# One operand in PSUM for the last batch's Strassen sums, q's pair sums and low halves of the later heads, with a new order table

## The chip, the cores and the metric

The kernel runs on one core of a Trainium2 chip. A core has TensorE (PE: matmuls; PEld is its weight loads), VectorE (DVE), ScalarE (ACT), GpSimd (POOL) and SyncE (SP, which issues the DMAs here). SBUF is the large on-chip memory, PSUM the small one of eight banks that TensorE writes and that DVE and ACT also read and write (no POOL instruction of this kernel does). The metric is the device time of one execution in microseconds, as the median of several runs.

## The reference

```python
B, H, S, D = 4, 8, 1152, 64              # q, k, v: (B, H, S, D), float32
q_pool = q.reshape(B, H, S // 2, 2, D).mean(axis=3)           # 576 queries
scores = (q_pool @ k.transpose(0, 1, 3, 2)) / np.sqrt(D)
scores = scores - scores.max(-1, keepdims=True)
attn = np.exp(scores); attn = attn / (attn.sum(-1, keepdims=True) + 1e-09)
x = (attn @ v).transpose(0, 2, 1, 3).reshape(B * 576, H * D)  # 2304 x 512
gate = 1.0 / (1.0 + np.exp(-(x @ w_gate)))                    # 512 x 1536
return (gate * (x @ w_val)) @ w_out                           # 1536 x 512
```

## The kernel before

**Numbers.** Most operands are split into a high part in the matmul's reduced float32 format and a low part, the rest. A product is three matmuls: high by high, high by low, low by high. So every operand needs a high copy (ACT) and a subtraction for the low part (POOL or DVE).

**Attention.** The 32 heads run one after the other, in pairs that share an x tile. `head_operands` (from line 479) loads a head's q and k, forms the sum of each pair of queries on POOL (q_sum, line 504, 64x576), its high half twice on ACT (line 509), the low half (line 514, on DVE for heads 16 to 31, on POOL for the earlier ones), k's high halves on ACT (line 524) and its low halves (line 530; the second of the two on DVE for heads 16 to 31, by KLD). `maxima` multiplies transposed scores on TensorE (line 553) and reduces them on DVE (line 559) into pm, the maximum of each query. The 576 queries are two halves of 288 columns. For each, `half` multiplies scores (line 671), ACT takes exponentials (675, 704), DVE forms the low part el (707), TensorE multiplies by v (714, 718), and POOL adds up the denominators (736, 743, 746). `normalise` divides (transposes and reciprocal on DVE, a product on POOL) and splits the result into x (lines 842 and 846).

**Gated layer.** After the heads of a batch come that batch's gate, value and output products, line 970, mixed into the heads of the next batch. Weights come from DRAM in tiles wg and wo (lines 1005, 984). The gated low part of g is formed on POOL (1209). In the last batch, after which no heads are left to mix with, the gate and value products use Strassen's scheme with seven products instead of eight. `differences` forms four differences of blocks of x (T1 to T4): sums on DVE (line 882), high halves on ACT (871), low halves on DVE (875). `combinations` forms four sums of weight blocks (S1 to S4): two full sums of 128x512 (line 1028), four mixes of 128x256 (1031), both on DVE with all operands in the tile kr, then highs on ACT (1044) and lows on POOL (1048). `seven` multiplies (line 1082), keeps a first result (ACT, 1100), adds others to it (DVE, 1092 and 1128), and `two_rows` takes tanh (1141), the product with the gate (1151) and its split (1155, 1158).

**Order.** Nothing is scheduled by the compiler. Every operation is registered with `pl.op` (engine, estimated time, due time, what it follows, which tiles it takes), and at the end `Plan.placed` puts all operations in the order of a stored table, ORDER; a second one, PLACES, says which buffer of its tag each tile gets. Each engine runs its own instructions in that order, and semaphores between engines follow from the tiles. So an instruction that waits holds up all that stands behind it on its engine. Of the buffers that matter here there are 8 PSUM banks (tag b), 1 kr, 1 vr, 2 wo, 3 wg, 3 sg, 2 r, 2 y, 2 t and 1 acc.

## Time and profile before

| what | value |
|---|---|
| median of 3 runs | 918.13 us (917.62 to 918.35) |
| the profiled execution | 919.11 us |
| its span | 917.3 us |
| PE busy | 894.9 us, 98% |
| DVE busy | 749.6 us, 82% |
| POOL busy | 714.1 us, 78% |
| ACT busy | 671.2 us, 73% |

The span runs from the first to the last instruction in the trace; the profiled execution's own time is 1.8 us more. PE's busy time counts a pipelined matmul until its end, so a busy PE can still have issued less than it could; the number of matmuls in a window tells more. DVE, POOL and ACT are busy for most of the time beside it and matter where PE waits for them.

### The profile page before, as it was taken

What the parts mean: (1) busy time and instruction counts of PE and PEld (TensorE: products, weight loads), DVE (VectorE), ACT (ScalarE), POOL (GpSimd) and SP (SyncE); (2) the same over time, 40 slices, a digit from 0 to 9 for tenths busy, and PEclk for the clock granted to TensorE, in tenths of its full rate; (3) what the DMA queues carried; (4) which work ended last, traced back from release to release, by engine and by line L of the source; (5) the groups of instructions that cost most, each with busy time, mean ns of one, the idle gap of its engine ahead of it and who ended that gap; (6) DMA issues with size and microseconds to landing.
All of it is one profiled execution on the core that took longest, in us unless ns stands there. A gap on an engine that the chain in (4) does not pass through costs nothing.

```text
span 917.3 us, 18691 instructions
## 1 busy us (share of the span) xinstructions
PE 894.9 (98%) x6251; PEld 869.0 (95%) x6251; DVE 749.6 (82%) x1605; ACT 671.2 (73%) x1747; POOL 714.1 (78%) x711
## 2 busy tenths in 40 slices
PE   7999999999999999999999999999999989999998
PEld 6888889999999999999999999999999979889997
DVE  7888869898998979788687778878787888998964
ACT  4999989999998776778876777787778646544421
POOL 7676658998998889899889889989798768745521
PEclk9999999999999999999999999999999989999999
DMA  7899887978868666536345453555544213456313
GB/s 193 255 282 286 266 222 227 276 247 251 294 203 262 200 171 190 165 104 185 123 153 154 105 168 119 181 176 166 148 132 151 88 54 108 144 185 209 136 64 126
DMA packets 57856, 164.40 MB, mean 179 GB/s; under 512 B 16864, under 2 KB 21216, under 8 KB 52000
## 3 DMA queue, kind: packets, MB, share of 16 engines
q1 hardware_dynamic: 57600, 162.91, 57.5%
...
q10 hardware_dynamic: 160, 0.30, 0.1%
...
## 4 chain that ended last, share of the span: by engine, by line
PE 83%; DVE 9%; DMA 3%; issue 2%; POOL 1%; ACT 1%; SPq 0%; DVEq 0%; ACTq 0%; POOLq 0%
PE bank L970 37%; PE bank L671 16%; PE bank L553 8%; PE bank L689 7%; PE bank L718 6%; PE bank L714 6%; PE bank L1082 2%; DVE kr L1031 2%; DVE kr L1028 1%; DMA wo<-wo_d 1%; PE bank L794 1%; DVE bank L1128 1%; DMA vt<-wg_d 1%; DVE sg L1092 1%; DVE el L707 1%
## 5 line engine op out<-in xcount | busy, mean ns | idle before, releaser
L970 PE MATMUL bank<-x,wg 128*128 128x288 f32 x1728 | 289.5, 296 | 0.5 <-DVE pm L559 0.5
L970 PEld LDWEIGHTS bank<-x,wg 128*128 128x128 f32 x1728 | 254.2, 188 | 0.8 <-DVE pm L559 0.7
L559 DVE TENSOR_REDUCE pm<-bank 128x1 f32<-128x384 f32 x375 | 199.4, 551 | 43.0 <-PE bank L553 38.9
L675 ACT ACTIVATE eh<-bank 128x288 fp32r<-128x288 f32 x432 | 171.7, 410 | 85.7 <-PE bank L671 50.2
L707 DVE TENSOR_TENSOR el<-bank,eh 128x288 fp32r<-128x288 f32 x432 | 187.5, 451 | 45.1 <-ACT bank L704 24.1
L970 PE MATMUL bank<-g,wo 128*128 128x288 f32 x1152 | 188.1, 296 | 3.1 <-DMA wo<-wo_d 1.2
L671 PE MATMUL bank<-QA,KA 128*128 128x288 f32 x576 | 172.0, 305 | 1.1 <-DVE el L707 1.1
L704 ACT ACTIVATE bank<-bank 128x288 f32<-128x288 f32 x432 | 170.8, 407 | 0.2
L970 PEld LDWEIGHTS bank<-g,wo 128*128 128x128 f32 x1152 | 165.6, 188 | 5.7 <-ACT t L1141 1.3
L671 PE MATMUL bank<-QB,KB 128*128 128x288 f32 x576 | 166.4, 295 | 0.3 <-DVE QB L384 0.3
L736 POOL TENSOR_TENSOR acc<-acc,eh 128x576 f32<-128x576 f32 x92 | 134.5, 1462 | 16.1 <-ACT eh L675 12.4
L553 PE MATMUL bank<-KA,QA 128*128 128x384 f32 x375 | 125.0, 353 | 4.3 <-DVE pm L559 4.1
L718 PE MATMUL bank<-el,vt 128*128 128x288 f32 x432 | 117.3, 295 | 0.9 <-DVE el L707 0.9
L671 PEld LDWEIGHTS bank<-QA,KA 128*128 128x128 f32 x576 | 108.5, 188 | 5.0 <-DVE el L707 1.7
L714 PE MATMUL bank<-eh,vt 128*128 128x288 f32 x432 | 110.3, 296 | 1.3 <-DVE el L707 0.8
L671 PEld LDWEIGHTS bank<-QB,KB 128*128 128x128 f32 x576 | 108.5, 188 | 1.7 <-DVE QB L384 0.6
L718 PEld LDWEIGHTS bank<-el,vt 128*128 128x128 f32 x432 | 78.2, 188 | 1.2 <-DVE el L707 1.2
L714 PEld LDWEIGHTS bank<-eh,vt 128*128 128x128 f32 x432 | 76.4, 188 | 2.1 <-DVE el L707 1.0
L689 PE MATMUL bank<-e,ve 128*128 128x288 f32 x288 | 77.9, 406 | 0.0
L530 POOL TENSOR_TENSOR KB<-kr,KA 64x576 fp32r<-64x576 f32 x46 | 67.6, 1475 | 12.0 <-ACT KA L524 5.8
L553 PEld LDWEIGHTS bank<-KA,QA 128*128 128x128 f32 x375 | 68.8, 188 | 7.1 <-DVE pm L559 4.7
L736 POOL TENSOR_TENSOR acc<-eh,eh 128x576 f32<-128x576 f32 x48 | 68.8, 1433 | 8.4 <-ACT eh L675 7.0
(142 smaller groups left out, 1605.7 us busy)
## 6 DMA issues: line engine op xcount, KB each, us to landing
...
```

The lines of the kernel that those rows point to most:

```text
L530: e.tensor_tensor(out=tl(kh)[1][HI, s], in0=tl(kr)[HI, s], in1=tl(kh)[0][HI, s].bitcast(F32), op=ALU.subtract)
L553: nc.tensor.matmul(out=tl(m)[LO if t == 4 else ALL, 0:384], lhsT=lhs(t), rhs=rhs()[:, j * 384:(j + 1) * 384], start=True, stop=True)
L559: nc.vector.tensor_reduce(out=o, in_=tl(m)[p, 0:384], axis=AXX, op=ALU.max)
L671: nc.tensor.matmul(out=tl(m)[:, 0:GN], lhsT=tl(hd["k"])[k][:, ks], rhs=tl(hd["q"])[k][:, a:b], start=(k == 0), stop=(k == 1))
L675: nc.scalar.activation(out=ev(), in_=tl(m)[:, 0:GN], func=ACTF.Exp, scale=1.0 / 16.0)
L689: nc.tensor.matmul(out=tl(av[0])[:, 0:GN], lhsT=pair(c, 0), rhs=tl(h), start=(c == 0), stop=(c == NC - 1))
L704: nc.scalar.activation(out=p, in_=p, func=ACTF.Exp, scale=1.0 / 16.0)
L707: nc.vector.tensor_tensor(out=tl(el), in0=tl(m)[:, 0:GN], in1=ev().bitcast(F32), op=ALU.subtract)
L714: nc.tensor.matmul(out=tl(av[0])[:, 0:GN], lhsT=pair(c, w), rhs=ev(), start=(c == 0), stop=(c == NC - 1))
L718: nc.tensor.matmul(out=tl(av[1])[:, 0:GN], lhsT=pair(c, 1 - w), rhs=tl(el), start=(c == 0), stop=(c == NC - 1 and not mine_c))
L736: nc.gpsimd.tensor_tensor(out=tl(acc), in0=tl(old).bitcast(F32), in1=tl(eh).bitcast(F32), op=ALU.add)
L970: nc.tensor.matmul(out=ps[:, 0:GN], lhsT=l, rhs=r, start=(n == 0 and j == 0), stop=(n == 3 and j == 2))
```

## The change

Four places form sums with one operand in a PSUM bank where both were in SBUF.

- Heads 16 to 31, q (QPS): for each half of 288 columns ACT copies one query of each pair into a bank, DVE adds the other there, ACT takes the high half from it twice, DVE subtracts with the bank as one operand. POOL's sum is gone.
- Heads 16 to 31, k (KLD): POOL forms the low half of the first 640 columns, ACT copies the last 512 into a bank, and DVE subtracts with that as one operand.
- `differences`: ACT copies the high part of a block into a bank, and every sum and low half on DVE has a bank as one operand; two banks are held for each block.
- `combinations`: ACT copies the right half of a weight block into a bank, DVE adds its low part there, POOL adds the left halves in kr, the four mixes have one operand in a bank, and ACT copies two results back into kr for POOL's lows. Two banks are held.

In `seven` the products come in another order, adds write into the product's own bank (`plus_in`), and the second set of a block keeps its sums in r tiles; in odd rows the factors are in y. ORDER and PLACES are new for the whole program (one pair of lines of the table stands here). TensorE's instructions stay the same in number; DVE gets 46 more, ACT 132, POOL 8. New line numbers: 882 becomes 922 and 942, 875 becomes 935, 1028 and 1031 become 1090 and 1099, 559 is 607, 707 is 755, 970 is 1030, 1082 is 1182, 1201 is 1303.

```diff
 ORDER = (
-    "c-jrugM#2X006)mX_^!%)3a?Gd$w)cw(oZLY}>YN+qP}KH-9k_BQpx4GJw$-$QX>yU<NT3!!RbpF(UIwWSL@&zz`;69ELI;<1#*zkV(e`Od=))"
+    "c-jrsQ-jz_06^hn;!H9zW|GwQ*0#A@TU*<1x3+EDwr$(C?cVzb&f|A@N}xnaqGSqE3Z+vjrBR47DT*>EhGMBl9H5F(9A#4u<x+%7Or@mKQyxWA"
...
-        a = pl.op("POOL", pool(SQ), q_sum, at, after=[lq], uses=[qr])
-        qa = pl.op("ACT", act(SQ), lambda: q_hi(0, LO), at, after=[a], uses=[qr], take=[qh])
-        ql = pl.op(on, pool(SQ) if on == "POOL" else 0.95, q_lo, at, after=[qa], uses=[qr, qh])
-        qb = pl.op("ACT", act(SQ), lambda: q_hi(1, HI), at + 4, after=[a], uses=[qr, qh])
...
+            bk = pl.hold("b")
+            ps = lambda: tl(bk)[LO, 0:GN]
+            def copy():
+                nc.scalar.activation(out=ps(), in_=tl(qr)[:, 1, a:b], func=ACTF.Copy)
+            def add():
+                nc.vector.tensor_tensor(out=ps(), in0=ps(), in1=tl(qr)[:, 0, a:b], op=ALU.add)
+            def high(k, p):
+                nc.scalar.activation(out=tl(qh)[k][p, a:b], in_=ps(), func=ACTF.Copy)
+            def low():
+                qa = tl(qh)[0]
+                nc.vector.tensor_tensor(out=qa[HI, a:b], in0=ps(), in1=qa[LO, a:b].bitcast(F32), op=ALU.subtract)
+            o = pl.op("ACT", act(GN), copy, at + 0.2 * hf, after=[lq] + c0, uses=[qr] + ([qh] if hf else []),
+                      take=[bk] if hf else [bk, qh])
+            c0.append(o)
+            s_ = pl.op("DVE", dve(GN), add, at + 0.2 * hf, after=[o], uses=[qr, bk])
+            h = pl.op("ACT", act(GN), lambda: high(0, LO), at + 0.2 * hf, after=[s_], uses=[bk, qh])
+            h2 = pl.op("ACT", act(GN), lambda: high(1, HI), at + 0.5 + 0.2 * hf, after=[s_], uses=[bk, qh])
+            return h, h2, pl.op("DVE", dve(GN), low, at + 0.2 * hf, after=[h], uses=[bk, qh])
...
-            by = "DVE" if k and KLD(u) else "POOL"
-            def k_lo(s=s, by=by):
-                e = nc.vector if by == "DVE" else nc.gpsimd
-                e.tensor_tensor(out=tl(kh)[1][HI, s], in0=tl(kr)[HI, s], in1=tl(kh)[0][HI, s].bitcast(F32),
-                                op=ALU.subtract)
...
+        if KLD(u):
+            bk, far = pl.hold("b"), slice(SK - 512, SK)
+            def k_copy():
+                nc.scalar.activation(out=tl(bk)[HI, 0:512], in_=tl(kr)[HI, far], func=ACTF.Copy)
+            def k_far():
+                nc.vector.tensor_tensor(out=tl(kh)[1][HI, far], in0=tl(bk)[HI, 0:512], in1=tl(kh)[0][HI, far].bitcast(F32),
+                                        op=ALU.subtract)
+            kb.append(pl.op("POOL", pool(SK - 512), lambda: k_lo(slice(0, SK - 512)), at + 6, after=ka, uses=[kr, kh]))
+            a = pl.op("ACT", act(512), k_copy, at + 6.1, after=[ka[1]], uses=[kr], take=[bk])
+            kb.append(pl.op("DVE", dve(512), k_far, at + 6.1, after=[a, ka[1]], uses=[bk, kh]))
...
-        old, fh = xs[p - 2, 0], tb["f"]
-        t1 = lambda: tl(fh).rearrange("p c d -> p (c d)")[:, GN * j:GN * j + GN]
-        b1 = lambda l, g: tl(old)[:, l, GN * g:GN * g + GN].bitcast(F32)
-        b21, b22 = (lambda: tl(me)[:, 0:GN]), (lambda: tl(me)[:, GN:SQ])
-        def split(n, src, uses, after, at):
-            h = tb[n]
+        old, fh, right, mixed = xs[p - 2, 0], tb["f"], pl.hold("b"), pl.hold("b")
+        ps = lambda h: tl(h)[:, 0:GN]
+        part = lambda l, g: tl(old)[:, l, GN * g:GN * g + GN].bitcast(F32)
+        left = lambda: tl(fh).rearrange("p c d -> p (c d)")[:, GN * j:GN * j + GN]
+        def whole(h, g, out, uses, take):
+            def high():
+                nc.scalar.activation(out=ps(h), in_=part(0, g), func=ACTF.Copy)
+            def low():
+                nc.vector.tensor_tensor(out=out(), in0=ps(h), in1=part(1, g), op=ALU.add)
+            o = pl.op("ACT", act(GN), high, s - 2, after=[x_done[p - 2, g], nm], uses=[old], take=[h])
+            return pl.op("DVE", dve(GN), low, s - 2, after=[o], uses=[old, h] + uses, take=take)
...
-                t = t_block(h, j)
-                nc.vector.tensor_tensor(out=t[:, 1], in0=src(), in1=t[:, 0].bitcast(F32), op=ALU.subtract)
...
+                o = t_block(t, j)
+                nc.vector.tensor_tensor(out=o[:, 1], in0=ps(h), in1=o[:, 0].bitcast(F32), op=ALU.subtract)
...
-        o = mix(t1, lambda: b1(0, 1), lambda: b1(0, 0), ALU.subtract, [old] + ([fh] if j else []),
-                [x_done[p - 2, 0], x_done[p - 2, 1]], s - 2, [] if j else [fh])
-        o = mix(t1, t1, lambda: b1(1, 1), ALU.add, [old, fh], [o], s - 2)
...
+        mine = lambda g: lambda: tl(me)[:, GN * g:GN * g + GN]
+        r, m = (lambda: ps(right)), (lambda: ps(mixed))
+        b12 = whole(right, 1, r, [], [])
+        b11 = whole(mixed, 0, left, [fh] if j else [], [] if j else [fh])
+        t1 = less(mixed, r, left, [right, fh], [b12, b11], s - 1.9)
+        t3 = less(right, mine(1), r, [me], [t1, nm], s)
+        s1 = split("1", mixed, [t1], s)
+        t2 = less(mixed, mine(1), m, [me], [s1, nm], s + 0.1)
+        s2 = split("2", mixed, [t2], s + 0.1)
+        split("3", right, [t3], s + 0.2)
+        t4 = less(mixed, mine(0), m, [me], [s2], s + 0.3)
+        split("4", mixed, [t4], s + 0.3)
...
-            fh, sh = pl.hold("kr"), pl.hold("K")
-            f0, f1 = 0, 512
+            fh, sh, bk = pl.hold("kr"), pl.hold("K"), [pl.hold("b"), pl.hold("b")]
             L, R, A = slice(0, 256), slice(256, 512), slice(0, 512)
-            def full(w, h):
-                nc.vector.tensor_tensor(out=f(h, A), in0=w(0, s, A).bitcast(F32), in1=w(1, s, A).bitcast(F32), op=ALU.add)
+            def f(k, cols):
+                return tl(bk[k])[:, cols]
+            def high(k, w):
+                nc.scalar.activation(out=f(k, R), in_=w(0, s, R).bitcast(F32), func=ACTF.Copy)
+            def low(k, w):
+                nc.vector.tensor_tensor(out=f(k, R), in0=f(k, R), in1=w(1, s, R).bitcast(F32), op=ALU.add)
+            def left(k, w):
+                nc.gpsimd.tensor_tensor(out=tl(fh)[:, 256 * k:256 * k + 256], in0=w(0, s, L).bitcast(F32),
+                                        in1=w(1, s, L).bitcast(F32), op=ALU.add)
+            f0, f1 = (lambda: tl(fh)[:, 0:256]), (lambda: tl(fh)[:, 256:512])
             def mix(out, in0, in1, op, after):
-                return pl.op("DVE", dve(256), lambda: nc.vector.tensor_tensor(out=f(*out), in0=f(*in0), in1=f(*in1), op=op),
-                             at - 6, after=after, uses=[fh])
-            r0 = pl.op("DVE", dve(512), lambda: full(a0, f0), at - 7, after=[l0], uses=w0, take=[fh])
-            r1 = pl.op("DVE", dve(512), lambda: full(a1, f1), at - 7, after=[l1], uses=w1 + [fh])
-            s1 = mix((f1, R), (f1, L), (f1, R), ALU.add, [r1])
-            s3 = mix((f1, L), (f0, L), (f1, L), ALU.subtract, [r0, s1])
-            s2 = mix((f0, L), (f1, R), (f0, L), ALU.subtract, [s1, s3])
-            s4 = mix((f0, R), (f0, R), (f0, L), ALU.subtract, [s2])
+                return pl.op("DVE", dve(256), lambda: nc.vector.tensor_tensor(out=out(), in0=in0(), in1=in1(), op=op),
+                             at - 6, after=after, uses=bk + [fh])
+            full, first_high = [], []
+            for k, (w, a, l) in ((1, (w1, a1, l1)), (0, (w0, a0, l0))):
+                o = pl.op("ACT", act(256), lambda k=k, a=a: high(k, a), at - 7, after=[l, x_done[NP - 2, 1]] + first_high, uses=w,
+                          take=[bk[k]] + ([fh] if k else []))
+                first_high.append(o)
+                full.append(pl.op("POOL", pool(256), lambda k=k, a=a: left(k, a), at - 7, after=[l] + first_high[:1], uses=w + [fh]))
+                full.append(pl.op("DVE", dve(256), lambda k=k, a=a: low(k, a), at - 7, after=[o], uses=w + [bk[k]]))
+            s1 = mix(lambda: f(1, L), lambda: f(1, R), f1, ALU.add, full[0:2])
+            s2 = mix(f0, lambda: f(1, L), f0, ALU.subtract, [s1, full[2]])
+            s3 = mix(lambda: f(1, R), lambda: f(1, R), f0, ALU.subtract, [s2])
+            s4 = mix(lambda: f(0, R), lambda: f(0, R), f0, ALU.subtract, [s2, full[3]])
...
+            o = pl.op("ACT", act(512), high_s(0, lambda: f(1, A)), at - 6, after=[s1, s3], uses=[bk[1]], take=[sh])
+            c = copied(lambda: tl(fh)[:, 512:1024], lambda: f(1, A), [o])
+            done = [pl.op("POOL", pool(512), low_s(0, 512), at - 6, after=[o, c], uses=[fh, sh])]
+            c = copied(f1, lambda: f(0, R), [s4, s1])
+            o = pl.op("ACT", act(512), high_s(1, lambda: tl(fh)[:, 0:512]), at - 6, after=[c, s2], uses=[fh, sh])
+            done.append(pl.op("POOL", pool(512), low_s(1, 0), at - 6, after=[o], uses=[fh, sh]))
...
-            s1, s2, s4 = (pl.hold("sg") for _ in range(3))
-            def mult(wname, name):
+            if s == 0:
+                th = [pl.hold("sg") for _ in range(3)]
+                s1, s2, s3 = [(h, slice(0, GN)) for h in th]
+            else:
+                r0, r1 = pl.hold("r"), pl.hold("r")
+                s1, s2, s3 = (r0, slice(0, GN)), (r0, slice(GN, SQ)), (r1, slice(0, GN))
...
-            b, p, at = mult("A11", "11")
-            k1 = keep(s1, b, [p], at)
-            b, p, at = mult("S2", "T2")
-            k2 = plus(s2, b, s1, [p, k1], at)
-            b, p, at = mult("A12", "21")
-            put(0, 0, b, s1, [p, k1], at)
...
+            a, p, at = mult("A11", "11", in_row)
+            k1 = keep(s1, a, [p], at)
+            a, p, at = mult("A12", "21", [k1])
+            put(0, 0, a, plus_in(a, a, s1, [p, k1], at), at)
+            b, p, at = mult("S2", "T2", [k1])
+            u2 = plus(s2, b, s1, [p, k1], at)
+            in_row[:] = [u2]
+            d, p, at = mult("S1", "T1", [k1])
+            u4 = plus(s3, d, s2, [p, u2], at)
+            c, p, at = mult("S3", "T3", [k1])
+            u3 = plus(s2, c, s2, [p, u2, u4], at)
+            put(1, 1, c, plus_in(c, c, s3, [p, u4, u3], at), at)
+            d, p, at = mult("S4", "22", [u2])
+            put(0, 1, d, plus_in(d, d, s3, [p, u4], at), at)
+            e, p, at = mult("A22", "T4", [u2])
+            put(1, 0, e, plus_in(e, e, s2, [p, u3], at), at)
...
-            gh, fg = [pl.hold("g") for _ in range(2)], [[pl.hold("acc")] * 2, [pl.hold("t"), pl.hold("t")][::-1]]
+            gh = [pl.hold("g") for _ in range(2)]
+            fg = [[pl.hold("y")] * 2, [pl.hold("y")] * 2] if i % 2 else [[pl.hold("acc")] * 2, [pl.hold("t"), pl.hold("t")][::-1]]
```

How the order changes, at three places. In the names a number behind the underscore is a tile's; x is a batch's attention output, y a pair's output before the split, vr a value tile that `differences` borrows, el and eh the low and high parts of exponentials, pm the maxima, bank any PSUM bank.

DVE, the first block's differences, about 743 us into the span. Before:

```order
L570 TENSOR_REDUCE pp0_114<-pp0_114 128x1
L559 TENSOR_REDUCE pm1_113<-bank_69 128x1
L875 TENSOR_TENSOR QA2_82<-vr0_88,QA2_82 128x288
L559 TENSOR_REDUCE pm1_113<-bank_69 128x1 x2
L1201 SCALAR_TENSOR_TENSOR sg0_142<-sg0_142,bank_69 128x288
L707 TENSOR_TENSOR el0_95<-bank_69,eh3_94 128x288
L559 TENSOR_REDUCE pm1_113<-bank_69 128x1 x3
L882 TENSOR_TENSOR vr0_88<-x7_128 128x288
```

After:

```order
L922 TENSOR_TENSOR bank_69<-bank_69,x6_127 128x288
L755 TENSOR_TENSOR el3_98<-bank_69,eh0_91 128x288
L922 TENSOR_TENSOR vr0_88<-bank_69,x6_127 128x288
L942 TENSOR_TENSOR bank_69<-bank_69,vr0_88 128x288
L942 TENSOR_TENSOR bank_69<-y0_118,bank_69 128x288
L755 TENSOR_TENSOR el1_96<-bank_69,eh3_94 128x288
L607 TENSOR_REDUCE pm1_113<-bank_69 128x1
L1303 SCALAR_TENSOR_TENSOR sg0_142<-sg0_142,bank_69 128x288
L935 TENSOR_TENSOR KP_116<-bank_69,KP_116 128x288
```

The low half that stood among the reductions of the maxima (line 875) stands later, behind more of the next head's el, and each sum names a bank.

DVE, the first combinations of weights, near 772 us. Before:

```order
L1028 TENSOR_TENSOR kr0_86<-wg1_133 128x512
L1031 TENSOR_TENSOR kr0_86<-kr0_86 128x256 x2
L707 TENSOR_TENSOR el2_97<-bank_69,eh3_94 128x288
L1031 TENSOR_TENSOR kr0_86<-kr0_86 128x256
L1201 SCALAR_TENSOR_TENSOR sg1_143<-sg1_143,bank_69 128x288
L1031 TENSOR_TENSOR kr0_86<-kr0_86 128x256
L707 TENSOR_TENSOR el3_98<-bank_69,eh3_94 128x288
```

After:

```order
L1090 TENSOR_TENSOR bank_69<-bank_69,wg0_3382 128x256
L1099 TENSOR_TENSOR bank_69<-bank_69,kr0_86 128x256
L1099 TENSOR_TENSOR kr0_86<-bank_69,kr0_86 128x256
L1090 TENSOR_TENSOR bank_69<-bank_69,wg2_134 128x256
L1099 TENSOR_TENSOR bank_69<-bank_69,kr0_86 128x256 x2
L755 TENSOR_TENSOR el1_96<-bank_69,eh0_91 128x288
L1303 SCALAR_TENSOR_TENSOR sg1_143<-sg1_143,bank_69 128x288
```

The 512-column sum is gone; a 256-column sum into a bank and the mixes stand in one row, no el between them.

TensorE, the last output products, from 903 us. wo0_135 and wo1_136 are the two wo buffers, each loaded again for the next four products. Before:

```order
L970 MATMUL bank_69<-g3_1466,wo0_135 128x288 x6
L970 MATMUL bank_69<-g0_1463,wo1_136 128x288 x3
L970 MATMUL bank_69<-g1_1464,wo1_136 128x288 x3
L970 MATMUL bank_69<-g0_1463,wo1_136 128x288 x3
L970 MATMUL bank_69<-g2_1465,wo1_136 128x288 x3
L970 MATMUL bank_69<-g3_1466,wo1_136 128x288 x3
L970 MATMUL bank_69<-g1_1464,wo1_136 128x288 x3
L970 MATMUL bank_69<-g2_1465,wo1_136 128x288 x3
L970 MATMUL bank_69<-g3_1466,wo1_136 128x288 x3
L970 MATMUL bank_69<-g0_1463,wo0_135 128x288 x3
```

After:

```order
L1030 MATMUL bank_69<-g3_1485,wo0_135 128x288 x6
L1030 MATMUL bank_69<-g2_1484,wo1_136 128x288 x3
L1030 MATMUL bank_69<-g0_1482,wo1_136 128x288 x3
L1030 MATMUL bank_69<-g1_1483,wo1_136 128x288 x3
L1030 MATMUL bank_69<-g3_1485,wo1_136 128x288 x3
L1030 MATMUL bank_69<-g2_1484,wo1_136 128x288 x3
L1030 MATMUL bank_69<-g3_1485,wo1_136 128x288 x3
L1030 MATMUL bank_69<-g0_1482,wo0_135 128x288 x3
```

Between the last use of wo0_135 and its next one stood 24 matmuls, now 18.

## Rows read from the trace of the kernel before

**Rows 1.** The page's first part: busy time, share of the span and instructions of each engine.

```profile
PE 894.9 (98%) x6251; PEld 869.0 (95%) x6251; DVE 749.6 (82%) x1605; ACT 671.2 (73%) x1747; POOL 714.1 (78%) x711
```

**Rows 2.** Windows: start:end and length (us), busy time and instructions by engine, granted clock, DMA.

```profile
300.00:350.00 50.00, 50.00 (x370) 49.74 (x369) 41.50 (x92) 40.38 (x111) 42.37 (x44) 1.00 0.53 160
650.00:700.00 50.00, 50.00 (x372) 50.00 (x371) 37.54 (x85) 38.21 (x106) 41.83 (x41) 1.00 0.47 141
700.00:750.00 50.00, 45.45 (x326) 44.69 (x325) 42.26 (x85) 30.06 (x83) 37.59 (x40) 0.96 0.28 97
750.00:800.00 50.00, 46.32 (x329) 44.77 (x328) 42.98 (x79) 30.97 (x87) 37.99 (x35) 0.97 0.34 117
800.00:850.00 50.00, 47.00 (x344) 45.53 (x343) 46.92 (x97) 20.13 (x48) 25.69 (x22) 1.00 0.55 192
850.00:917.00 67.00, 62.39 (x457) 60.57 (x455) 43.92 (x98) 17.92 (x43) 23.97 (x24) 1.00 0.32 105
```

**Rows 3.** Windows after 740 us, columns as above.

```profile
742.00:753.00 11.00, 6.52 (x29) 6.00 (x30) 9.60 (x15) 3.17 (x10) 5.22 (x8) 0.69 0.00 0
748.20:752.50 4.30, 4.22 (x17) 4.22 (x18) 3.35 (x9) 1.14 (x3) 0.00 (x0) 0.50 0.00 0
774.00:794.00 20.00, 16.32 (x114) 15.00 (x113) 19.51 (x35) 12.57 (x34) 15.55 (x15) 1.00 0.32 110
804.00:810.00 6.00, 4.58 (x33) 4.12 (x32) 5.80 (x11) 2.44 (x7) 3.04 (x2) 1.00 0.51 162
810.00:874.00 64.00, 62.05 (x457) 60.54 (x456) 60.09 (x126) 27.34 (x66) 35.48 (x32) 1.00 0.49 171
898.00:914.00 16.00, 14.89 (x105) 13.79 (x103) 6.36 (x15) 1.63 (x4) 2.42 (x3) 1.00 0.40 122
```

**Rows 4.** Timeline of 742 to 749 us: start, us, engine, line, what, idle before.

```profile
742.95 4.81 DVE L875 TENSOR_TENSOR QA<-vr,QA 128x288 fp32r<-128x288 f32 x1
745.15 2.29 POOL L846 TENSOR_TENSOR x<-y,x 128x288 fp32r<-128x288 f32 x3
748.28 0.69 PE L553 MATMUL bank<-KA,QA 128*128 128x384 f32 x1 [3.83 <-DVE pm L559]
```

**Rows 5.** Timeline of 776 to 779 and 805 to 809 us, DVE and TensorE.

```profile
776.06 1.33 DVE L1031 TENSOR_TENSOR kr<-kr 128x256 f32<-128x256 f32 x1
778.18 0.40 PE L671 MATMUL bank<-QA,KA 128*128 128x288 f32 x1 [0.70 <-DVE el L707]
805.48 2.62 DVE L882 TENSOR_TENSOR y<-y,x 128x288 f32<-128x288 f32 x2
808.52 0.53 PE L1082 MATMUL bank<-QB,wg 128*128 128x288 f32 x2 [1.42 <-DVE QB L875]
```

**Rows 6.** Line 882 alone: count, shortest, median and longest in ns, first and last start.

```profile
L882 DVE TENSOR_TENSOR vr<-vr,x x4: 442/1322/1666, 738.8 to 758.3; 128x288 f32<-128x288 f32 x4
```

**Rows 7.** Groups by line and form: count, busy us, mean ns of one, idle before.

```profile
L707 DVE TENSOR_TENSOR el<-bank,eh 128x288 fp32r<-128x288 f32 x432 | 187.5, 451 | 45.1 <-ACT bank L704 24.1 <-PE bank L718 13.4 <-ACT eh L675 2.9
L1031 DVE TENSOR_TENSOR kr<-kr 128x256 f32<-128x256 f32 x48 | 28.2, 588 | 0.9
L1028 DVE TENSOR_TENSOR kr<-wg 128x512 f32<-128x512 f32 x18 | 17.3, 973 | 0.8 <-POOL KB L1048 0.8
L514 DVE TENSOR_TENSOR QA<-qr,QA 64x576 fp32r<-64x576 f32 x16 | 17.4, 1086 | 0.8
L530 DVE TENSOR_TENSOR KB<-kr,KA 64x576 fp32r<-64x576 f32 x16 | 16.9, 1057 | 0.7 <-ACT KA L524 0.2
L675 ACT ACTIVATE eh<-bank 128x288 fp32r<-128x288 f32 x432 | 171.7, 410 | 85.7 <-PE bank L671 50.2 <-PE bank L714 16.8 <-issue 4.9
L509 ACT ACTIVATE QA<-qr 64x576 fp32r<-64x576 f32 x31 | 21.0, 677 | 5.7 <-POOL qr L504 5.1 <-issue 0.5
L504 POOL TENSOR_TENSOR qr<-qr 64x576 f32<-64x576 f32 x31 | 44.0, 1420 | 11.9 <-DMA qr<-in_qT_dram 6.2 <-ACT r L758 4.5 <-DVE pm L466 0.9
```

**Rows 8.** Timeline of the tail, TensorE.

```profile
910.53 3.46 PE L970 MATMUL bank<-g,wo 128*128 128x288 f32 x24 [0.34 <-DMA wo<-wo_d]
```

More of the change, by code (lines that the diff above doesn't have):

```diff
@@ L369, in attention_glu_kernel @@
     KLD = lambda u: u >= 16
+    QPS = lambda u: u >= 16
     NMP = lambda p: True
@@ L1091, in add @@
                 def add():
-                    nc.vector.tensor_tensor(out=tl(out), in0=tl(bank)[:, 0:GN], in1=tl(sh), op=ALU.add)
-                return pl.op("DVE", dve(GN), add, at - 1, after=after, uses=[bank, sh],
-                             take=[] if out is sh else [out])
+                    nc.vector.tensor_tensor(out=part(out), in0=tl(bank)[:, 0:GN], in1=part(sh), op=ALU.add)
+                uses, take = first_use(out)
+                return pl.op("DVE", dve(GN), add, at - 1, after=after, uses=[bank] + ([] if sh[0] is out[0] else [sh[0]]) + uses, take=take)
@@ L1097, in keep, with plus_in, add @@
+            def plus_in(out, bank, sh, after, at):
+                def add():
+                    nc.vector.tensor_tensor(out=tl(out)[:, 0:GN], in0=tl(bank)[:, 0:GN], in1=part(sh), op=ALU.add)
+                return pl.op("DVE", dve(GN), add, at - 1, after=after, uses=[bank, sh[0]] + ([] if out is bank else [out]))
             def keep(out, bank, after, at):
                 def copy():
-                    nc.scalar.activation(out=tl(out), in_=tl(bank)[:, 0:GN], func=ACTF.Copy)
-                return pl.op("ACT", act(GN), copy, at - 1, after=after, uses=[bank], take=[out])
@@ L1116, in seven @@
-            put(0, 1, b, s4, [p, k4], at)
-            b, p, at = mult("A22", "T4")
-            put(1, 0, b, s2, [p, u2], at)
+                    nc.scalar.activation(out=part(out), in_=tl(bank)[:, 0:GN], func=ACTF.Copy)
+                uses, take = first_use(out)
+                return pl.op("ACT", act(GN), copy, at - 1, after=after, uses=[bank] + uses, take=take)
+            a, p, at = mult("A11", "11", in_row)
+            k1 = keep(s1, a, [p], at)
+            a, p, at = mult("A12", "21", [k1])
@@ L1132, in factor, with put_gate @@
             def factor(r, hf):
                 f = tl(fg[r][hf])
+                if i % 2:
+                    return f[:, GN * hf:GN * hf + GN]
                 return f[:, hf] if r == 0 else f
-            def put_gate(r, hf, bank, sh, after, at):
+            def put_gate(r, hf, bank, o, at):
                 f = fg[r][hf]
-                new = r == 1 or (r, 1 - hf) not in done
+                new = (r == 1 and i % 2 == 0) or (r, 1 - hf) not in done
                 def tanh():
                     nc.scalar.activation(out=factor(r, hf), in_=tl(bank)[:, 0:GN], func=ACTF.Tanh, scale=0.5)
-                o = add(bank, sh, after, at)
@@ L1159, in lo @@
                                             op=ALU.subtract)
-                o = add(bank, sh, after, at)
                 o = pl.op("DVE", dve(GN), mult, at - 1, after=[o, done[r, hf]], uses=[f, bank])
```

416 lines of the change are left out of this document (213 added, 203 removed).

## The prediction

> **What bounds the kernel now.** I read the page's busy line first [rows 1]: TensorE is busy for 98% of the span, so only its gaps can be won. The windows of 50 us show where those are [rows 2]: a full window holds 372 matmuls, 50 / 372 = 0.134 us each, and from 300 to 700 next to nothing is missing. From 700 on, where the last heads end and the last batch's Strassen products begin, windows hold 326, 329 and 344. That is 46 + 43 matmuls at 0.134 and 32 at 0.133 (against 376), 12.0 + 4.3 = 16.3 us; the last window's 457 stand against 480 up to the last matmul's end at 914, 3.1 us more. In all 19.4 us of TensorE issue are lost after 700.
>
> The finer windows put the loss into places [rows 3], each counted as window / 0.134 minus the matmuls that ran: 742 to 753: 82 - 29 = 53, 7.1 us. 774 to 794: 149 - 114 = 35, 4.7 us. 804 to 810: 45 - 33 = 12, 1.6 us. 810 to 874: 478 - 457 = 21, 2.8 us. 898 to 914: 119 - 105 = 14, 1.9 us. Together 18.1 of the 19.4.
>
> Then the timeline of the first place [rows 4]. One DVE subtraction of 128x288 of line 875, both operands in SBUF, runs from 742.95 to 747.76; the last of a row of POOL instructions, started 745.15 and 2.29 us long, ends at 747.44. The maxima reduction of line 559 stands behind it in DVE's queue, and the next transposed score matmul of line 553 waits 3.83 us for that. A form of line 882 of the same size takes 0.442 us at its shortest, 1.322 in the median and 1.666 at its longest [rows 6], so it is not the work that is long: a DVE instruction with two SBUF operands is held while POOL runs. Afterwards TensorE runs at half of its clock (granted 0.50, that is 1.2 GHz) from 748.20 to 752.50 [rows 3]; before that it had stood idle for the 3.83 us. That slow stretch is half of the 4.3 us, about 2.1 us of the 7.1, and goes only when the wait goes.
>
> The Trainium skill says what the lock is (SBUF — State Buffer, "Who interferes with whom"): a DVE instruction with two SBUF inputs contends with a GpSimd instruction that reads SBUF, whoever issues first holds the port, and with at most one SBUF input there is no contention. The trace agrees on who is held, but not on how long: by that rule the wait would be one POOL instruction, where the row of 4.81 us outlasts several. By the rule alone the first place would give about 0.8 us and its clock loss, not 7.1; I keep the row.
>
> The later places show the same in smaller pieces [rows 5]: line 1031, 128x256, takes 1.33 us at 776.06, and a score matmul at 778.18 waits 0.70 us for the el of line 707 queued on DVE; two sums of line 882 take 2.62 us at 805.48, and the product of line 1082 then waits 1.42 us at 808.52.
>
> **The change, part by part.** The change gives nearly every two-SBUF tensor_tensor on DVE one operand in PSUM. What such a form costs is shown by line 707, one operand in PSUM, 432 times beside a busy POOL: mean 0.451 us for 288 columns [rows 7], no more than the undisturbed two-SBUF form (0.442). So I price 288 columns at 0.45 and do not expect a hold.
>
> Differences (lines 875, 882; after: one PSUM bank pair per block). Twenty DVE instructions stay twenty, at 0.45 each = 9.0 us, and four ACT copies of 288 columns come in, at the 0.41 of line 675 [rows 7] = 1.6 us. What goes is the hold, and with it the 3.83 us wait and the slow clock. In the new order the first low halves also stand behind el of the next head, where one stood among the reductions before. I give 6.5 of the 7.1 us as won; the 0.6 left is for reductions that wait a little for any DVE neighbour. If POOL still held DVE, nothing is won.
>
> Combinations (lines 1028, 1031, 1044, 1048). Removed on DVE: 48 x 0.588 = 28.2 and 18 x 0.973 = 17.3 us [rows 7], and six more of the 512-column form at the same price, 5.8: 51 us. Added: 72 of 256 columns with one PSUM operand. No row has that width; line 707's 0.451 for 288 columns is the upper bound, 72 x 0.451 = 32 us, 256 / 288 of it, 29, the lower. DVE wins some 19 us between 760 and 876, where in one stretch it was busy for 60.09 of 64 us [rows 3]. POOL gets 24 sums of 256 columns: by the 576-column sum of line 504, 1.420 us [rows 7], 256 columns cost 1.42 x 256 / 576 = 0.63, bounds 0.63 and 1.42, 15 to 34 us; I take 0.7, since the form has some fixed part, 17 us. It has room: 35.48 of 64 us busy there [rows 3]. ACT gets 36 copies of 256 columns at up to 0.41 and 12 of 512 at 0.41 to 0.82, 20 to 25 us, beside 27.34 of 64 busy. Both engines are idle for about half of that stretch, so these costs lie beside the products, but each combination is now a chain ACT, DVE, ACT, POOL with more hand-overs; that is where a wait may return. Of the 4.7 us at 774 to 794 I count 3.5 as won: the order puts the last normalisation, its differences and the first products close together there, and about 1 us stays exposed. Of the 1.6 at 804 to 810, 1.4; of the 2.8 at 810 to 874, 1.8, since part of them are waits for accumulation adds (0.45 each) that stay.
>
> Heads 16 to 31. POOL loses the pair sum, 16 x 1.420 = 22.7 us; its low half grows by 64 columns, 16 x 0.16 = 2.5. DVE loses 16 x 1.086 + 16 x 1.057 = 34.3 [rows 7] and gets 64 x 0.451 + 16 x (0.45 to 0.90) = 36 to 43. ACT loses 32 x 0.677 = 21.7 and gets 96 x 0.41 + 16 x (0.41 to 0.82) = 46 to 52: about +28 us net, 1.7 us per head. In 650 to 700 ACT is busy for 38.21 of 50 us, in 300 to 350 for 40.38 [rows 2], and TensorE lacks nothing there, so 10 to 12 us of each window cover it. I cost this part at nothing; uncovered it would be the whole 28 us.
>
> Products. The seven products of a block, their adds and tanhs stay the same in number; second sets keep their sums in r tiles, odd rows their factors in y, both free by then, and products come in another order. The new after= entries of mult bind the table, not the chip, where TensorE waits for tiles. I cost this at nothing; what hides the adds is the next product, 6 x 0.134 = 0.8 us, against 0.45.
>
> The tail. Before, TensorE waits 0.34 us at 910.53 for a wo load into a buffer that 24 matmuls earlier, 3.2 us, was released [rows 8]; in the new order only 18 matmuls, 2.4 us, stand between. The load is issued 0.8 us nearer to its use: +0.8 us, between 0 (if the buffer is free as early as before) and 1.6 (if both last loads wait so).
>
> Before 700 TensorE loses little, and the order is new there: between -1.5 and +1.5 us, taken as -0.6, since fewer DVE instructions are held.
>
> Sum: -6.5 - 3.5 - 1.4 - 1.8 + 0.8 - 0.6 = -13.0 us. The profiled run took 919.11 us (span 917.3), 0.98 above the median of the runs shown: 919.11 - 13.0 = 906.1, and by the median 918.13 - 13.0 = **905.1**.
>
> A second rule of the skill speaks against the change (VectorE: DVE Perf Modes, the section on the TRN2 errata): a VectorE instruction costs 58 cycles plus its columns from SBUF, 120 from PSUM, at 0.96 GHz, 65 ns more. The rows deny it, 0.442 to 0.451 us. By the page, 92 instructions of the last batch would give back 6 us of DVE time, an estimate.
>
> **The rivals.** First, half of the gain: the pressure moves to the longer chain of a combination. For it: two PSUM banks are held through each combination and each block of differences, and POOL forms one more operand; against it: POOL and ACT idle for half of 810 to 874. Then 774 to 794 and 810 to 874 keep their waits, and the sum is -6.5 - 1.4 + 0.8 = -7.1, 911 us.
>
> Second, the better end: all places empty and the tail no worse, -18.1, 900 us. Against it: the new order has chains of its own.
>
> Third, slower: ACT becomes the bound in heads 16 to 31. The new copies and highs, 1.7 us net per head, stand in the same queue as the exponentials of line 675, which DVE's el and then TensorE wait for. It decides once more than 13.0 / 16 = 0.8 us of the 1.7 per head comes through to TensorE; with 1.1 it gives 16 x 1.1 - 13.0 = +4.6, 922.7 us. Against it: ACT's 10 idle us per window.
>
> Fourth, the change doesn't do what it says: POOL holds the PSUM forms too. Then the hold stays and the extra instructions come on top, 918 us. Against it stands the mean of line 707.
>
> **How the numbers follow.** The forecast (902 to 908) has 0.50, the better end (898 to 902) 0.13, half the gain (908 to 916) 0.23, no effect 0.06, slower 0.08. A measurement of this kernel can tell about 0.2%, 1.8 us, from no change. Faster is thus 0.50 + 0.13 + 0.23 = 0.86, same 0.06, slower 0.08. The range 899 to 913 holds the forecast, most of the better end and most of half the gain, 0.8.
>
> **What would show it.** Right: the DVE forms of the new lines at 0.41 to 0.46 us with their longest below 0.6; no half clock and 80 matmuls in each 11 us around 742; windows after 700 with 365 or more; DVE's busy time down by some 30 us, ACT's up by about 50. Wrong: windows between 300 and 700 below 368 with waits for ACT (third rival); products that wait for POOL's lows of a combination, or for a bank (first); new forms above 1 us beside POOL (fourth). The tail term is wrong if the last wo load is not waited for longer than 0.34 us.

## The result

The changed kernel takes 896.92 us in the median (895.70 to 897.78), the kernel before 918.24 in the same comparison: a ratio of 0.9767, 95% interval 0.9750 to 0.9784, so 21.3 us less. The forecast was 905.1 with a range from 899 to 913; the direction was right, the gain 8.2 us larger than forecast. The profiled execution took 895.70 us, its span is 893.9, 23.4 less than before. Executions of the changed kernel fall on levels about 1.2 us apart (895.7 at a granted clock of 1.000, 896.9 and more at 0.996 to 0.998), the profiled one on the lower, and one execution of a later run, mix_more, at a granted clock of 0.754, is left out of that run's median.

The page's first line and the windows of the changed kernel (columns as in [rows 2] and [rows 3]):

```profile
PE 884.4 (99%) x6251; PEld 865.5 (97%) x6251; DVE 720.2 (81%) x1651; ACT 714.0 (80%) x1879; POOL 692.6 (77%) x719
```

```profile
250.00:300.00 50.00, 50.00 (x371) 50.00 (x370) 46.60 (x107) 45.61 (x120) 46.39 (x46) 1.00 0.76 249
450.00:500.00 50.00, 50.00 (x372) 50.00 (x371) 41.26 (x99) 42.59 (x118) 42.30 (x44) 1.00 0.52 151
700.00:750.00 50.00, 50.00 (x373) 50.00 (x372) 40.02 (x95) 36.70 (x105) 39.38 (x41) 1.00 0.35 118
750.00:800.00 50.00, 50.00 (x380) 50.00 (x379) 39.64 (x101) 36.59 (x100) 40.29 (x43) 1.00 0.48 166
800.00:850.00 50.00, 50.00 (x379) 50.00 (x378) 39.07 (x100) 32.45 (x83) 37.49 (x43) 1.00 0.50 175
742.00:753.00 11.00, 11.00 (x85) 11.00 (x84) 7.20 (x17) 8.71 (x27) 10.11 (x13) 1.00 0.27 97
774.00:794.00 20.00, 20.00 (x153) 20.00 (x152) 18.39 (x49) 11.97 (x31) 15.98 (x17) 1.00 0.65 220
804.00:810.00 6.00, 6.00 (x48) 6.00 (x47) 5.34 (x15) 4.61 (x12) 4.13 (x6) 1.00 0.85 254
810.00:874.00 64.00, 64.00 (x484) 64.00 (x484) 44.31 (x110) 33.22 (x83) 38.72 (x42) 1.00 0.38 133
874.00:890.00 16.00, 15.10 (x114) 14.87 (x113) 7.32 (x18) 1.78 (x4) 3.22 (x4) 1.00 0.39 122
```

The windows compare the same times, not the same work: near 800 us the changed kernel is some 17 us further on (the 5500th matmul starts at 789.4 us instead of 806.3). Against [rows 2], no window between 700 and 850 lacks a matmul: 373, 380 and 379 where 326, 329 and 344 ran. Against [rows 3], 742 to 753 holds 85 instead of 29 at full clock, 810 to 874 holds 484 instead of 457, and DVE is busy there for 44.31 us instead of 60.09. The only place left is the tail, 114 of 119 in 874 to 890. Before 700 some came too: 371 and 372 matmuls in the windows from 250 and 450, where the kernel before has these rows:

```profile
250.00:300.00 50.00, 49.10 (x364) 48.89 (x363) 44.16 (x98) 43.89 (x111) 46.00 (x45) 1.00 0.78 242
450.00:500.00 50.00, 49.55 (x364) 49.17 (x363) 38.62 (x86) 36.12 (x97) 44.52 (x42) 1.00 0.47 150
```

Cut at 290 us, the kernel before and then the changed one up to 700:

```profile
0.00:290.00 290.00, 284.44 (x1790) 265.16 (x1790) 247.00 (x531) 259.85 (x646) 229.57 (x241) 1.00 0.82 247
290.00:700.00 410.00, 409.28 (x3014) 408.31 (x3015) 326.55 (x720) 312.22 (x842) 359.25 (x351) 1.00 0.52 160
```

```profile
0.00:290.00 290.00, 284.97 (x1812) 267.30 (x1813) 249.82 (x538) 263.89 (x654) 230.60 (x242) 1.00 0.84 251
290.00:700.00 410.00, 410.00 (x3022) 409.18 (x3021) 329.61 (x767) 334.82 (x919) 332.31 (x341) 1.00 0.53 157
```

The first instruction of the new forms starts at 291.2 us (line 529). Up to there every engine's instructions are those of the kernel before; only their order and the buffers differ. So the 22 matmuls more before 290, 2.9 us at 0.134 each, came with the order alone; the 8 more from there to 700 are 1.1 us.

The new DVE forms by line (count, shortest, median, longest in ns, first and last start), and the tail's wait in the timeline:

```profile
L942 DVE TENSOR_TENSOR bank<-y,bank x6: 445/452/455, 738.1 to 787.9; 128x288 f32<-128x288 f32 x6
L942 DVE TENSOR_TENSOR bank<-bank,vr x2: 466/466/467, 737.7 to 779.2; 128x288 f32<-128x288 f32 x2
L1099 DVE TENSOR_TENSOR bank<-bank,kr x36: 422/424/433, 762.6 to 853.8; 128x256 f32<-128x256 f32 x36
L539 DVE TENSOR_TENSOR QA<-bank,QA x32: 450/451/452, 295.9 to 701.5; 64x288 fp32r<-64x288 f32 x32
L579 DVE TENSOR_TENSOR KB<-bank,KA x16: 686/694/696, 306.3 to 700.2; 64x512 fp32r<-64x512 f32 x16
```

```profile
883.73 6.64 PE L1030 MATMUL bank<-g,wo 128*128 128x288 f32 x48 [0.90 <-DMA wo<-wo_d]
```

All these forms are short, the longest of 288 columns 0.467 us, where the four of line 882's 14 instructions that [rows 6] shows had a median of 1.322 and a longest of 1.666.

### The profile page after: what moved, and what is told of

Its sections match the earlier page's. It is cut to its first block, busy times and chain, and to the rows that moved or that the text cites. A ratio compares the mean times of both kernels' runs of the same rounds, so it can differ in the third digit from the quotient of the medians.

```text
span 893.9 us, 18887 instructions
## 1 busy us (share of the span) xinstructions
PE 884.4 (99%) x6251; PEld 865.5 (97%) x6251; DVE 720.2 (81%) x1651; ACT 714.0 (80%) x1879; POOL 692.6 (77%) x719
## 4 chain that ended last, share of the span: by engine, by line
PE 98%; DVE 2%; DMA 0%; issue 0%; DVEq 0%
PE bank L1030 42%; PE bank L719 17%; PE bank L601 8%; PE bank L737 8%; PE bank L1182 7%; PE bank L766 6%; PE bank L762 6%; PE bank L842 1%; DVE pm L471 1%; PE bank L1359 1%; DVE QB L389 0%; DMA wo<-wo_d 0%; PE bank L769 0%; DVE KB L1406 0%; DVE pm L607 0%; PE bank L466 0%
## 5 line engine op out<-in xcount | busy, mean ns | idle before, releaser
L607 DVE TENSOR_REDUCE pm<-bank 128x1 f32<-128x384 f32 (+1 forms) x375 | 199.4, 551 | 43.0 <-PE bank L601 39.5
L784 POOL TENSOR_TENSOR acc<-acc,eh 128x576 f32<-128x576 f32 x92 | 131.8, 1433 | 28.0 <-ACT eh L723 25.3
L601 PE MATMUL bank<-KA,QA 128*128 128x384 f32 x375 | 122.7, 351 | 0.1
L784 POOL TENSOR_TENSOR acc<-eh,eh 128x576 f32<-128x576 f32 x48 | 68.8, 1432 | 24.6 <-ACT eh L723 21.3
L564 POOL TENSOR_TENSOR KB<-kr,KA 64x576 fp32r<-64x576 f32 (+1 forms) x46 | 67.4, 1474 | 10.3 <-PE bank L719 5.3
```

Of the source, the lines that this page charges most:

```text
L564: nc.gpsimd.tensor_tensor(out=tl(kh)[1][HI, s], in0=tl(kr)[HI, s], in1=tl(kh)[0][HI, s].bitcast(F32), op=ALU.subtract)
L601: nc.tensor.matmul(out=tl(m)[LO if t == 4 else ALL, 0:384], lhsT=lhs(t), rhs=rhs()[:, j * 384:(j + 1) * 384], start=True, stop=True)
L607: nc.vector.tensor_reduce(out=o, in_=tl(m)[p, 0:384], axis=AXX, op=ALU.max)
L784: nc.gpsimd.tensor_tensor(out=tl(acc), in0=tl(old).bitcast(F32), in1=tl(eh).bitcast(F32), op=ALU.add)
```

## The experiments

All times are medians of three to ten executions. The kernel before gave 917.9 to 918.6 beside them, the changed kernel 896.9 and, measured again beside low_twice, headdiff_flat and tail_again, 896.8.

**1. Back into SBUF, one part each.** The order, the engines and the instructions stay those of the changed kernel; only the place of the partial sums moves.

```diff
-        ps = lambda h: tl(h)[:, 0:GN]                       # differences: a bank
+        ps = lambda h: SB["right" if h is right else "mixed"]   # SBUF, 288 columns each
...
-                return tl(bk[k])[:, cols]                   # combinations
+                return SB[f"sum{k}"][:, cols]
...
-            ps = lambda: tl(bk)[LO, 0:GN]                   # heads; k_far likewise
+            ps = lambda: SB["q"][LO, a:b]
```

> The changed kernel, but the two PSUM parts of differences (lines 919 to 942) are SBUF tiles of 288 columns; order, engines and number of instructions are those of the changed kernel. Theory H (POOL holds a DVE instruction with two SBUF operands, and that hold was the loss): the 20 DVE forms of these lines, 0.45 us each after the change, get rows of 1 us and more, and TensorE waits for el or maxima between 735 and 795 again; in the kernel before these places cost 7.1 + 1.6 us, so +3 to +9 us on 897. Rival O (the new order table brought the gain, the place of the operand little): within 1 us of 897. Rival L (the gain comes from the DVE time that went to ACT and POOL): within 1 us as well, since that stays moved.

> The changed kernel, but the two PSUM parts of combinations (lines 1087 to 1127) are SBUF tiles; order, engines and number of instructions as in the changed kernel. Theory H: of the 72 DVE forms (0.424 us in the median, longest 0.433) a good part gets 1 us and more beside POOL's 48 instructions there, TensorE waits between 760 and 870; before, 774 to 794 and 810 to 874 cost 4.7 + 2.8 us, so +3 to +8 us on 897. Rivals O and L: within 1 us of 897.

> The changed kernel, but the PSUM parts of q's pair sums and of k's far low half in heads 16 to 31 (lines 529 to 579) are SBUF tiles; all else as in the changed kernel. Theory H: the 80 DVE forms get long beside POOL (up to 1.5 us, 0.45 to 0.69 now), but heads 16 to 31 lost nothing to speak of in the kernel before either, with 32 such forms of 1.06 us; so +0 to +3 us on 897. Rival O: within 1 us.

Measured: differences 899.9 (+3.0), heads 914.5 (+17.6), combinations 908.2 (+11.3). In this last run one pair of SBUF tiles serves all combinations, and the order lets one begin before the one ahead is done with its sums, which are then overwritten; so it was made again with two sets in turn:

> The changed kernel with the PSUM parts of 11 of the 12 combinations in SBUF, two sets in turn so that no combination waits for the one before it as it could in the first such run; the second combination stays in PSUM, and in every other one the sums are rounded to the matmul's format. If the 11.3 us of the first run came from the hold on DVE: +7 to +11 us on 897, and DVE forms of 1 us and more. If they came from sharing one set: +0 to +3 us.

Measured 902.8 (+5.8): about half of the 11.3 was the sharing. The heads were the surprise, since the same heads lost next to nothing before. The timeline of head_flat shows the hold, and the view of its line 582 (579 in the changed kernel) how often:

```profile
310.27 0.29 POOL L658 TENSOR_TENSOR QB<-ident,pp 64x64 fp32r<-64x64 f32 x1
310.34 2.90 DVE L582 TENSOR_TENSOR KB<-q,KA 64x512 fp32r<-64x512 f32 x1
310.52 0.80 POOL L1314 TENSOR_TENSOR g<-sg,g 128x288 fp32r<-128x288 f32 x1
311.28 1.41 POOL L787 TENSOR_TENSOR acc<-acc,eh 128x576 f32<-128x576 f32 x1
312.76 1.13 POOL L794 TENSOR_TENSOR acc<-acc 128x288 f32<-128x288 f32 x1
313.79 0.67 PE L1033 MATMUL bank<-x,wg 128*128 128x288 f32 x3 [1.85 <-DVE el L758]
```

```profile
L582 DVE TENSOR_TENSOR KB<-q,KA x16: 689/765/2904, 310.3 to 719.7; 64x512 fp32r<-64x512 f32 x16
```

A subtraction of 512 columns, 0.69 us with its operand in PSUM, lasts 2.90, until 313.24; POOL's next two long instructions end at 311.32 and 312.69. The el of line 758 (707 before) waits behind it, and TensorE 1.85 us for that.

Not all of the 17.6 is hold, though. Around 294 us ACT's first copy into the new SBUF tile waits 3.96 us for a DMA out of the tile cs, a wait that the copy into a bank does not have, and head_flat (first window) issues 26 matmuls less there than the changed kernel (second), 3.5 us:

```profile
294.70 0.44 ACT L532 ACTIVATE q<-qr 64x288 f32<-64x288 f32 x1 [3.96 <-DMA wo_d<-cs]
```

```profile
290.00:300.00 10.00, 8.26 (x49) 8.03 (x48) 6.90 (x16) 5.41 (x15) 7.40 (x9) 0.83 0.97 377
```

```profile
290.00:300.00 10.00, 10.00 (x75) 10.00 (x74) 8.77 (x22) 7.72 (x22) 8.62 (x10) 1.00 0.96 372
```

That leaves 14.1 us for the heads. Every part loses time when its operands go back (theory H); neither the new order nor the work moved off DVE made these places cheap by itself (rivals O and L). To see whether the parts add up, heads and differences went back together:

> The changed kernel with the PSUM parts of the heads and of differences both in SBUF (the two runs of one part each gave +17.6 and +3.0). If the parts add up: +19 to +22 us on 897, 916 to 919, so that with the combinations' +5.8 the new order with all forms in SBUF would be slower than the kernel before, and the order alone brings nothing. If they share their waits: +17 to +18.

Measured 918.6 (+21.8, against 17.6 + 3.0 = 20.6). They add up; this run has the loss at 294 us too (47 matmuls in 290 to 300). Without that loss, and with the 5.8 of the combinations, the three parts are 14.1 + 3.0 + 5.8 = 22.9 us, about the 21.9 that lie between the kernels measured beside them. By this sum the new order with the operands in SBUF would stand about level with the kernel before; that kernel itself was not run.

**2. The hold in the old order.** POOL's low halves of x (line 846) cover 16 of 288 columns in the last batch; the rest is left out.

```diff
+            c = a + 16 if p >= 12 else b
-            nc.gpsimd.tensor_tensor(out=x[:, 1, a:b], in0=tl(st["y"])[:, a:b], ...
+            nc.gpsimd.tensor_tensor(out=x[:, 1, a:c], in0=tl(st["y"])[:, a:c], ...
```

> The kernel before, with its own order; POOL's low half of x (line 846) of the last batch covers 16 of 288 columns, so the rest of these low halves is left out. Theory H: the subtraction of line 875 at 743, 4.81 us long while POOL ran four such lows, is released some 2 us earlier and the wait of 3.83 us with its slow clock shrinks: -2 to -5 us on 918. If that instruction's length had another cause, nothing changes there: 918.

Measured 911.8 (-6.2). The window and the timeline of that place:

```profile
742.00:753.00 11.00, 10.47 (x73) 9.77 (x74) 9.91 (x24) 7.62 (x23) 6.50 (x12) 1.00 0.26 95
```

```profile
742.67 1.05 DVE L876 TENSOR_TENSOR QA<-vr,QA 128x288 fp32r<-128x288 f32 x1
743.37 0.43 POOL L847 TENSOR_TENSOR x<-y,x 128x16 fp32r<-128x16 f32 x1
```

POOL's lows take 0.43 or less there, the subtraction 1.05 instead of 4.81 us [rows 4], and 73 matmuls run where 29 did, 5.9 us, with the granted clock at 1.00 instead of 0.69. The first term of the sum, with its slow clock, is the hold.

**3. DVE time without a hold.** One more DVE instruction of 256 columns behind each mix, one operand in PSUM:

```diff
+                def twice():
+                    nc.vector.tensor_tensor(out=out(), in0=in0(), in1=in1(), op=op)
+                    nc.vector.tensor_tensor(out=f(1, L), in0=f(1, L), in1=ones, op=ALU.mult)
```

> The changed kernel with one more DVE instruction behind each of the 48 mixes of combinations (line 1099): 128x256, one operand in PSUM, multiplied by a tile of ones, at 0.42 us as its neighbours. That is 48 x 0.42 = 20 us of DVE between 760 and 856, about what the change had taken off DVE there; its length is certain, no hold in it. Theory H (the loss before was the hold, DVE's load alone is covered): +0 to +3 us on 897. Rival L (the loss was DVE's load, 60.09 of 64 us busy in 810 to 874): +5 to +8 us, most of the 9 us that were lost in 760 to 880.

Measured 913.4 (+16.4), more than either expected, for a reason beside the question: POOL, which fills the tile of ones, waited at 295 us, and TensorE for POOL (timeline of mix_twice):

```profile
295.16 0.32 POOL L284 MEMSET one<- 128x256 f32 x1 [7.86 <-DVE pm L610]
303.23 0.61 PE L722 MATMUL bank<-QB,KB 128*128 128x288 f32 x1 [6.85 <-POOL QB L392]
```

Made again with ones that cost nothing:

> As the run with one more DVE instruction behind each of the 48 mixes of combinations (+48 x 0.42 = 20 us of DVE between 760 and 856), but the ones come from a single column written at the start: in that run POOL waited 7.86 us near 295 to fill the tile of ones, and 72 matmuls, 9.6 us, were missing there, so that 16.4 - 9.6 = 6.8 us were left for the mixes. Theory D (in this stretch each us that DVE is busy longer costs TensorE a part of it, hold or no hold): +5 to +8 us on 897, all of it after 750. Theory H (only a hold costs): +0 to +3 us.

Measured 903.4 (+6.4 for 20.5 us of DVE). The opposite, less DVE time in the old order with the holds left in, by half of the columns of lines 1028 and 1031:

> The kernel before with the DVE sums of combinations on half of their columns (line 1028: 256 instead of 512, line 1031: 128 instead of 256); the other half of these sums is left out. DVE gets 24 x 0.26 + 48 x 0.14 = 13 us less between 760 and 876, as many holds as before. Theory D: a third to a half of that comes back, -4 to -6 us on 918. Theory H: -0 to -2 us.

Measured 911.1 (-7.5, more than theory D expected, for 12.5 us of DVE: line 1031 took 22.2 us in all instead of 28.2, line 1028 16.3 instead of 22.8). Its windows from 750 and 800 hold 348 and 371 matmuls where [rows 2] has 329 and 344:

```profile
750.00:800.00 50.00, 48.07 (x348) 47.12 (x347) 42.04 (x84) 31.79 (x90) 38.15 (x37) 0.97 0.35 124
800.00:850.00 50.00, 49.24 (x371) 48.94 (x370) 44.14 (x106) 22.91 (x54) 25.74 (x23) 1.00 0.56 196
```

And DVE time without a hold in the heads, the lows of lines 539 and 579 issued twice:

> The changed kernel with the DVE lows of heads 16 to 31 (lines 539 and 579) issued twice: +32 x 0.451 + 16 x 0.694 = 25.5 us of DVE between 295 and 702, with one operand in PSUM, so of certain length and without hold. Theory D (DVE time that the order has no room for comes out as TensorE waits, hold or no hold, at 0.3 to 0.6 us per us): +8 to +14 us on 897. Theory H (only the hold costs in the heads, whose 35 us more of DVE gave +17.6): +0 to +3 us.

Measured 905.7 (+8.9 for 25.5 us). Theory D holds in all three: 0.31, 0.60 and 0.35 us come or go for each microsecond of DVE time, without a hold in the first and the last. A doubled or halved instruction also makes its own chain longer or shorter, which these runs do not separate from DVE's load. Held time costs about as much as added time: 14.1 us for the 35.4 by which head_flat's three DVE lines are longer (0.40), 5.8 for 18.6 in comb_flat2 (0.31), 3.0 for 7.7 in diff_flat (0.39). And head_flat has more that is longer than DVE's lines: POOL is busy for 703.3 us instead of 692.6, and ACT's copies on the tile take 0.43 to 0.44 us instead of 0.39 to 0.40. So as far as these runs tell, the hold costs TensorE what any longer DVE instruction costs.

**4. ACT and POOL.** q's highs of heads 16 to 31 copied twice, in the changed kernel and in the one before; POOL's left sums issued twice:

> The changed kernel with the highs of q (line 535) of heads 16 to 31 issued twice: +64 x 0.40 = 26 us of ACT between 290 and 705, 1.6 us per head, on top of the 28 us that the change added. If ACT's idle time covers it, as the prediction costed that part at nothing: +0 to +2 us on 897. The prediction's third rival (ACT close to the bound in these heads): +8 us or more, with TensorE waiting for el behind late exponentials.

> The kernel before with q's two highs of heads 16 to 31 (line 509) copied once more in two halves each: +64 x 0.41 = 26 us of ACT between 290 and 720, in the old order. Theory F (an order table has room only for the instructions that it was made with; any more on an engine that TensorE's operands pass through comes out as TensorE waits): +5 to +12 us on 918, as the changed kernel's +11.7. Theory S (ACT's 10 to 14 idle us of 50 cover it; the changed kernel is special because ACT is fuller there): +0 to +2 us.

> The changed kernel with the left sums of combinations on POOL (line 1093, 0.738 us) issued twice: +24 x 0.738 = 17.7 us of POOL, and each combination's chain 0.74 to 1.5 us longer. If POOL's place in the chain has room, as the profile after says (38.72 of 64 us busy in 810 to 874), +0 to +1 us on 897. The prediction's first rival (the chain of ACT, DVE, ACT and POOL is near its limit): +3 us or more, with TensorE waiting for POOL's lows or for sums.

Measured: 908.7 (+11.8 for 26 us of ACT), 925.5 (+7.0 for 28 us), 902.6 (+5.7 for 17.7 us of POOL). Two windows of high_twice and one of left_twice:

```profile
450.00:500.00 50.00, 49.20 (x356) 48.12 (x355) 39.20 (x94) 44.21 (x123) 42.00 (x43) 1.00 0.46 144
650.00:700.00 50.00, 49.18 (x355) 47.95 (x354) 37.52 (x87) 42.29 (x117) 37.27 (x39) 1.00 0.52 156
```

```profile
810.00:874.00 64.00, 62.34 (x460) 60.96 (x459) 43.74 (x113) 33.38 (x86) 49.36 (x56) 1.00 0.39 135
```

ACT is idle for 6 and 8 us of 50, and TensorE still lacks 16 and 14 matmuls against the changed kernel. In 810 to 874 POOL is idle for 15 us of 64, and 460 ran instead of 484. Idle time of an engine was no cover for work that the order did not have. Theory F holds against S.

**5. The tail.** The last two wo loads go into K tiles that are free by then:

```diff
+                if kind == "wo" and m_ in (10, 11) and ch == B - 1:
+                    return TL["K"][0][m_ - 10][:, 0:1024].rearrange(...)
```

> The changed kernel, but the last two wo loads go to the K tile KA_74 and KB_77, whose last products end before the last Strassen product, instead of waiting for the wo buffers. The wait of 0.90 us at 883.73 for the wo load goes: -0.9 us on 897, 896.0. If the wait were the issue of the queue or the transfer itself and not the buffer, it stays at 897.

Measured 895.1, and again (tail_again, the same edit) beside the changed kernel itself (896.8) on the same chip 894.7. The wait for wo is gone; the timeline of tail_again shows the products with the last two loads without one:

```profile
882.73 3.34 PE L1030 MATMUL bank<-g,KA 128*128 128x288 f32 x24
885.91 3.34 PE L1030 MATMUL bank<-g,KB 128*128 128x288 f32 x24
```

Between executions on the same level the gain is 1.2 us (894.5 against 895.7, 895.7 against 896.9), not the medians' 2.1; 0.9 of it is that wait. With 0.9741 of the time before (0.9727 to 0.9756) it is the fastest version.

## Why the prediction was right and wrong

**The step that failed** is the sizing of four terms of the sum; the hold, the mechanism behind its largest term, stood. The spans of the profiled executions lie 23.4 us apart where 13.0 was forecast, 10.4 more (by the medians 8.2: the profiled execution before lies 0.98 above its median, the one after 1.22 below). The residues that I left standing in the four places make 3.0 of it, the tail 2.0, the time before 700 between 3.4 and 4.1, and 1.3 is the part of the loss after 700 (19.4 against 18.1) that I had put into no place and so left standing.

- **The bound and its places** were right: all that was won after 700 lay where the counts had it, but for that 1.3.
- **The hold** was right, and is shown from three sides: put back, in SBUF, in the new order; relieved in the old one; absent with one operand in PSUM (longest 0.467 us for 288 columns). The price of 0.45 for 288 columns held, 256 columns cost 0.424. The count did not: the differences are 22 DVE instructions before (8 of line 875, 14 of line 882) and 20 after, where I wrote that twenty stay twenty.
- **The residues were wrong.** I left 0.6, 1.2, 0.2 and 1.0 us of waits in the four places, on the ground that adds and a close chain stay exposed. They are all zero: 85, 153, 48 and 484 matmuls, 16.2 us won where 13.2 were counted. The forecast took waits of the old order for properties of the work, and priced DVE's win of 19 us at what single waits showed. The combinations' DVE sums went from 51.0 us (28.2 of line 1031, 22.8 of line 1028) to 30.7. At the 0.31 to 0.60 that mix_more and before_less_sums measured for each microsecond, those 20.3 us are worth 6 to 12 us, where the three later places held 9.1 in all and I counted 6.7 as won. comb_flat2, which puts 18.6 us of them back, loses 5.8. That the rest went by DVE time too, and not by the new order, is argued from these rates; no run separates the two.
- **The tail had the wrong sign.** I charged 0.8 us for 18 matmuls between two uses of a wo buffer. That wait did grow, from 0.34 [rows 8] to 0.90 us, and tail_k shows that it was the buffer; but all others near it went, 0.7 us are lost there now where it was 1.9.
- **Before 700** I took 0.6 us, for fewer held instructions, between -1.5 and +1.5. It is the term with the largest miss. The counts give 30 matmuls more up to 700, 4.0 us; as the remainder it is 4.7 (23.4, less the 19.4 - 0.7 = 18.7 that the counts explain after 700). The reason failed too: 22 of the 30 run before 290 us, where only the order had changed, and DVE's instructions took 0.465 us in the mean before and 0.464 after (247.00 us for 531, 249.82 for 538), so freed holds are not what brought them. What made the other 8 stays open.
- **Heads at nothing** came out right by luck, for a wrong reason. I let ACT's 10 idle us of 50 cover 1.7 us per head; high_twice shows that idle time does not do that, 26 us of ACT cost 11.8. The 26 us that the change adds in these heads (lines 529, 535 and 576 take 47.9 us, where line 509 took the 21.7 of the forecast) cost nothing that the windows show. The third rival's price is thus real for added work (0.46 per us). That the new table averted it, because it was made with these copies in it, is argued and not shown: the forms were not run in the old order.
- **The second rival**, all places empty and 900 us, was the case, with more on top; it had 0.13. The first rival's chain has no room to spare (left_twice) and no wait either. The rule on PSUM operands costing 65 ns more in the Trainium skill (VectorE: DVE Perf Modes, the section on the TRN2 errata) is again not borne out: 0.451 us with one operand in PSUM here, against 0.442 at the shortest with both in SBUF [rows 6].

What was not tried: the new forms in the old order, since the table belongs to its list of operations. So how the 21.3 us split between order and forms is not settled beyond two things: the 2.9 us before 290 came with the order alone, and with the forms put back the sum of the parts leaves about no gain.
